# A recurrence with a rounded two-pass matmul: difference tiles kept in PSUM, a fourth seven-product block in the third pair

## The chip, the cores and the metric

The kernel runs on one core of a Trainium2 chip. The metric is device time in microseconds (us) of one execution, as the median over runs. Shorter is better.

## The reference, cut to what matters

Two stages follow each other. The first is a recurrence along 6080 positions for two batches and 256 channels; the second is a dense layer pair with an ELU between the two matrix products.

```python
# x, f_logit: (2, 6080, 256)   lower_bound: (256)
sig = 1 / (1 + exp(-f_logit))
f = lower_bound + (1 - lower_bound) * sig
for t in range(6080):
    h = f[:, t] * h + (1 - f[:, t]) * x[:, t]
    y[:, t] = h
# y as (12160, 256); w_in: (256, 2048), w_out: (2048, 256)
h = y @ w_in
g = where(h > 0, h, exp(min(h, 0)) - 1)
out = g @ w_out
```

## The kernel before

**Tiling.** Everything is held transposed, with channels on the 128 partitions. The 6080 positions are cut into twelve stretches (SIZES, of 512 except for one of 448), and each stretch is taken for both batches at once: one such *pair* of position tiles, p from 0 to 11, named by the letters a to l. The 2048 inner channels are cut into eight *blocks* of 2 x 128, so a pair has eight blocks and the kernel has 96, numbered q = 8p + j. A block is a 2 x 2 problem: two tiles of inner channels (m) by two batches (t), and it takes 2 x 2 tiles of the input's channels. Its result is four tiles g(m, t) of 128 x 512, and the second matrix product adds them into four accumulators of the pair, acc(e, t), e being the tile of output channels.

**Precision.** Each operand is split into a rounded high part and the rest (names with h and l: gh and gl, wiH and wiL, yh and yl), and a product is three passes: high by high, low by high, high by low. ScalarE makes the high part with a cast; VectorE or GpSimd subtracts it from the value for the low part (`split`, `split_sum`, `operand`).

**First product.** From the thirteenth block on (q of 12 and more) the first matmul of a block is made with seven products M1 to M7 in place of eight (`quad`, L1137). They go into three PSUM tiles, x, v and z, which share four banks in turn (pool h). M1 goes to x, M3 to v, M4 to z; ScalarE copies x to SBUF as q, VectorE adds v and z to it; M5 is added to v, M2 to z, and these two sums are the tiles (0,1) and (1,0). Each goes through ELU (`elu`, L854: Exp and Relu on ScalarE, a max and subtraction on VectorE) into the SBUF tile g. Then M7 is added to v and M6 to z, and VectorE subtracts from q in place, in the bank (steps hv and hz). What stands there now are the *difference tiles*, which become (0,0) and (1,1). They go through ELU too (steps f0 and f1), with the result written to an SBUF tile hs; from the third pair on q carries a 1, so that f0 and f1 are one Exp and one min and max. After that the bank is free.

**Second product.** In an ordinary block (`second`, L965) the four g tiles are multiplied with the output weights in 24 matmuls: g is rounded as one 1024-wide tile (step s1), hs as another (step s2, written for GpSimd, though a mark in the order can give it to VectorE). In a *wide* block this product takes seven products too, 21 matmuls (`wide_product`, L997; P1 to P7). For them VectorE forms X (a tile of g less both tiles of hs, one 1024-wide step), Y1 and Y0. The first blocks of a pair are wide, `breadth` of them (L358): none in the first two pairs, three in the third, four in each later one. A wide block needs sums of its output weights, which `combine_out` (L652) makes once per block number; those of the fourth are made during the third pair, since there the fourth block is ordinary and uses the weights as they were. `chained` (L1200) ends the wide blocks of a pair together.

**End of a pair.** `store` (L1060) moves the accumulators out. In pairs with wide blocks the parts (e, t) other than (1,1) are added by VectorE to what is there already, and (1,1) is copied with a bias; in the last pair this copy is cut in two halves, one for ScalarE and one for VectorE (L1077), and each part leaves by a DMA of its own from SyncE.

**Order.** All steps are entered in a plan with the tiles they read and write, and a list written out by hand (ORDER, L66, 5239 entries) gives the one sequence in which they are issued; each engine runs its own steps in that sequence. An entry with a ~ goes to the other of VectorE and GpSimd. Costs and due times (`cost`, `want`, `late`) were for the planner that wrote the list and do nothing at run time. Steps of VectorE that work on SBUF alone and all steps of GpSimd are chained: where the engine changes from one to the next, the later one waits for the earlier (`lock`, `port`, at the end of the kernel). Steps of VectorE with a bank among their operands are outside that chain.

Of the kernel before, what the change touches and what calls it, by code (L numbers as in the profile page):

```python
# [7 lines left out]
F32 = mybir.dt.float32  # L8
# [42 lines left out]
FULL_FROM = 3  # L51
# [306 lines left out]
def breadth(p):  # L358

    return 0 if p < WIDE_FROM else WIDE - (p < FULL_FROM)  # L360

# [91 lines left out]
def kernel(  # L453
# [397 lines left out]

    def elu(q, group, j, src, src_names, want, psum, up=False):  # L854

        n = size(q)
        cnt = len(group["tiles"])
# [557 lines left out]
```

## Time and profile before

| | us |
|---|---|
| median of 3 runs | 973.31 |
| lowest and highest of them | 973.06 and 973.47 |
| the profiled execution | 973.24 |
| its span, first to last instruction | 971.5 |
| TensorE (PE) busy | 965.7 |
| VectorE (DVE) busy | 907.6 |
| ScalarE (ACT) busy | 808.3 |
| GpSimd (POOL) busy | 424.8 |

The span is the profiled execution from its first to its last instruction; the 1.74 us around it are not in the trace. A matmul's row lasts 0.39 us while the next starts 0.23 us after it, since matmuls are pipelined. So the busy time of PE says only that it is never empty, and how dense it is must be read from the spacing of starts and from the waits. A row of a shape group gives the mean time of one instruction. "Idle before" is the time that the engine stood still just ahead of the group's instructions, with the work that ended it.

### The profile page before, as it was taken

The page shows a single profiled execution, that of the slowest core. Times are in us where ns is not written, and L with a number is a line of the kernel's source. Part 1 is how long each engine was busy: PE and PEld are TensorE (multiplying, and loading weights), DVE is VectorE, ACT ScalarE, POOL GpSimd, SP SyncE. Part 2 cuts the span into 40 slices and gives each one's busy share as a digit, 9 for nine tenths or more (in the row PEclk, how much of TensorE's full clock was granted, in tenths as well). Part 3 has the DMA queues.
Part 4 walks back from the last instruction along what each step waited for, and adds up shares of the span by engine and source line. Part 5 has one row for each costly group of instructions (what it writes and reads, how often), then busy time and mean ns, then how long its engine had stood idle before and what let it go on. Part 6 is the DMA issues. An engine that isn't in the chain of part 4 may idle for free.

```text
span 971.5 us, 12644 instructions
## 1 busy us (share of the span) xinstructions
PE 965.7 (99%) x4283; PEld 800.8 (82%) x4283; DVE 907.6 (93%) x1305; ACT 808.3 (83%) x1304; POOL 424.8 (44%) x311
## 2 busy tenths in 40 slices
PE   9999999999999999999999999999999999999998
PEld 5788999888888888888888888888888888888886
DVE  7999999999899999999999999999999999998986
ACT  7899967898789789878888988978987887897865
POOL 0231124544663652563363364256346246436622
PEclk9999999999999999999999999999999999999999
DMA  6532100120002012011111100201201201010001
GB/s 216 174 119 78 54 1 1 39 86 1 6 39 87 1 44 86 1 44 48 41 44 43 45 15 29 88 1 43 88 1 44 75 14 44 22 65 23 23 1 44
DMA packets 10145, 46.55 MB, mean 48 GB/s; under 512 B 1248, under 2 KB 1248, under 8 KB 7520
## 3 DMA queue, kind: packets, MB, share of 16 engines
q1 hardware_dynamic: 9936, 45.75, 13.3%
q8 instruction: 33, 0.54, 0.2%
q14 instruction: 32, 0.26, 0.1%
q10 hardware_dynamic: 144, 0.00, 0.0%
HBM read 33.29 MB, written 12.45 MB: 47 GB/s over the span
## 4 chain that ended last, share of the span: by engine, by line
PE 98%; DMA 1%; ACT 1%; DVE 0%; SPq 0%; issue 0%
PE o L954 51%; PE hv L835 18%; PE hz L835 18%; PE hx L835 6%; DMA gl<-fx 1%; ACT gl L521 0%; PE h(_312 L835 0%; PE h(_389 L835 0%; PE h(_315 L835 0%; PE h(_400 L835 0%; PE h(_341 L835 0%; PE h(_955 L835 0%; PE h(_948 L835 0%; PE h(_936 L835 0%; PE h(_881 L835 0%; PE h(_862 L835 0%
## 5 line engine op out<-in xcount | busy, mean ns | idle before, releaser
L508 POOL TENSOR_TENSOR gl<-g,gh 128x1024 fp32r<-128x1024 f32 (+2 forms) x92 | 178.7, 1948 | 110.9 <-ACT gh L519 18.4
L519 ACT CAST gh<-g 128x1024 fp32r<-128x1024 f32 (+2 forms) x190 | 180.1, 952 | 45.9 <-DVE g L876 19.1
L835 PE MATMUL hz<-yo,wiH 128*128 128x512 f32 (+1 forms) x504 | 193.4, 388 | 0.0
L835 PE MATMUL hv<-yo,wiH 128*128 128x512 f32 (+1 forms) x504 | 192.5, 388 | 0.0
L954 PE MATMUL o<-gh,woL 128*128 128x512 f32 (+1 forms) x526 | 162.8, 386 | 0.0
L954 PE MATMUL o<-gh,woH 128*128 128x512 f32 (+1 forms) x526 | 162.3, 386 | 0.0
L954 PE MATMUL o<-gl,woH 128*128 128x512 f32 (+1 forms) x526 | 160.0, 386 | 0.0
L525 ACT ACTIVATE e<-e 128x512 f32<-128x512 f32 (+1 forms) x202 | 125.2, 626 | 3.9
L508 DVE TENSOR_TENSOR gl<-g,gh 128x1024 fp32r<-128x1024 f32 (+1 forms) x98 | 116.5, 1192 | 1.7 <-ACT gh L519 1.1
L954 PEld LDWEIGHTS o<-gl,woH 128*128 128x128 f32 x526 | 98.6, 188 | 19.4 <-DVE gl L508 0.2
L954 PEld LDWEIGHTS o<-gh,woL 128*128 128x128 f32 x526 | 98.7, 188 | 19.1 <-POOL woL L508 0.2
L954 PEld LDWEIGHTS o<-gh,woH 128*128 128x128 f32 x526 | 98.7, 188 | 19.1 <-ACT woH L519 0.2
L835 PEld LDWEIGHTS hv<-yo,wiH 128*128 128x128 f32 x504 | 94.6, 188 | 19.0
L835 PEld LDWEIGHTS hz<-yo,wiH 128*128 128x128 f32 x504 | 94.6, 188 | 19.0
L835 PE MATMUL hz<-yo,wiL 128*128 128x512 f32 (+1 forms) x252 | 97.8, 388 | 0.0
L835 PE MATMUL hv<-yo,wiL 128*128 128x512 f32 (+1 forms) x252 | 97.7, 388 | 0.0
L508 POOL TENSOR_TENSOR yo<-raw,yo 128x512 fp32r<-128x512 f32 (+1 forms) x38 | 49.1, 1296 | 109.8 <-DVE yo L508 46.8
L519 ACT CAST yo<-raw 128x512 fp32r<-128x512 f32 (+1 forms) x147 | 88.2, 615 | 9.4 <-DVE raw L761 4.2
L508 DVE TENSOR_TENSOR yo<-raw,yo 128x512 fp32r<-128x512 f32 (+1 forms) x109 | 72.0, 683 | 1.9 <-PE o L954 1.2
L525 ACT ACTIVATE e<-hv,units 128x512 f32<-128x512 f32 x80 | 54.9, 687 | 19.7 <-DVE hv L508 18.2
L508 POOL TENSOR_TENSOR ys<-raw 128x512 f32<-128x512 f32 x29 | 37.5, 1299 | 69.0 <-DVE raw L761 35.2
L525 ACT ACTIVATE e<-hz,units 128x512 f32<-128x512 f32 x80 | 55.0, 688 | 14.6 <-DVE hz L508 13.5
(382 smaller groups left out, 2075.2 us busy)
## 6 DMA issues: line engine op xcount, KB each, us to landing
raw<-fx SPq DMA_DIRECT2D x20, 1024.0 KB, 4.8
out_t<-v SPq DMA_DIRECT2D x20, 512.0 KB, 2.6
raw<-w SPq DMA_DIRECT2D x16, 512.0 KB, 4.7
raw<-fx SPq DMA_DIRECT2D x2, 896.0 KB, 4.5
gl<-fx SPq DMA_DIRECT2D x2, 512.0 KB, 6.1
out_t<-v SPq DMA_DIRECT2D x4, 256.0 KB, 2.2
out_t<-v SPq DMA_DIRECT2D x2, 448.0 KB, 3.8
gh<-fx SPq DMA_DIRECT2D x2, 256.0 KB, 4.4
```

The lines of the kernel that those rows point to most:

```text
L508: return e, cost, lambda: engines[e].tensor_tensor(out=out_(), in0=in0(), in1=in1(), op=op)
L519: nc.scalar.copy(out=out_(), in_=in_())
L525: nc.scalar.activation(out=out_(), in_=in_(), func=func, **args)
L835: nc.tensor.matmul(out=hb(q, b), lhsT=(wiH if m == "h" else wiL)[:, i, wi], rhs=T[kind, p, name], start=(start and j == 0), stop=(j == len ...
L954: nc.tensor.matmul(out=accs[p, e, t], lhsT=lhsT, rhs=rhs, start=(c == 1), stop=(c == total(p, e, t)), skip_group_check=True,)
```

## The change

- The fourth block of the third pair becomes wide, like the first three (FULL_FROM is 2, and `breadth` gives NARROW or WIDE, both four). The weight sums of the fourth block are made with those of the others, ahead of the third pair.
- In all blocks from the thirteenth on but the very last, the ELU of the difference tiles writes its result back into the bank (`stay`). The new `split_bank` rounds them from there, each tile for itself: a 512-wide cast by ScalarE and a 512-wide subtraction by VectorE per tile (steps t0 and t1) in place of step s2.
- In wide blocks X becomes two 512-wide steps that read the banks, and Y1 reads a bank too; both are VectorE's. Y0 is now kept in a tile of g. The bank is free after the last of these steps.
- The order is written anew (5465 entries). In it the last accumulator that PE completes is (1,1), whose copy is the one in halves; before it was (0,1). The planner's numbers for the last DMAs change.

The list of the order is cut to its first line; the rest of the diff is whole.

```diff
@@ -48,7 +48,8 @@
 
 WIDE = 4
 WIDE_FROM = 2
-FULL_FROM = 3
+FULL_FROM = 2
+NARROW = 4
 NPLAIN = MP + MIXED
 SECOND = [*range(MP - MIXED, MP), *range(MP - MIXED)]
 
@@ -63,285 +64,297 @@
 
 
 ORDER = (
-    " 0 3 4 5 6 7 8 9 10 11 12 13 14 15 16 17 18 19 20 21 22 23 24 25 26 27 28 29 30 31 32 33 34 35"
...
+    " 0 33 21 26 28 34 35 43 29 31 39 12 20 36 14 40 42 37 7 19 11 51 24 52 25 5 15 30 32 13 48 4"
...
 )
@@ -357,7 +370,7 @@
 
 def breadth(p):
 
-    return 0 if p < WIDE_FROM else WIDE - (p < FULL_FROM)
+    return 0 if p < WIDE_FROM else NARROW if p < FULL_FROM else WIDE
 
 
 def place(q):
@@ -851,7 +864,7 @@
 
 
 
-    def elu(q, group, j, src, src_names, want, psum, up=False):
+    def elu(q, group, j, src, src_names, want, psum, up=False, stay=False):
 
         n = size(q)
         cnt = len(group["tiles"])
@@ -865,6 +878,8 @@
             return t
 
         def gt():
+            if stay:
+                return src()
             t = tl(group["pool"], g, [P, group.get("slots", cnt), n])
             return t.rearrange("p c n -> p (c n)") if j is None else t[:, j]
 
@@ -875,8 +890,9 @@
                 "DVE", dve_cost(width), want + 1.3,
                 lambda: nc.vector.scalar_tensor_tensor(
                     out=gt(), in0=et(), scalar=1.0, in1=src(), op0=ALU.min, op1=ALU.max,
-                ), reads=src_names + [e], writes=[(g, j)], takes=[(group["pool"], g)],
-                lock=not psum,
+                ), reads=[e] + ([] if stay else src_names),
+                writes=src_names if stay else [(g, j)],
+                takes=[] if stay else [(group["pool"], g)], lock=not psum,
             )
             return
         act(width, want, et, src, func=ACTF.Exp, reads=src_names, writes=[e], takes=[(kind, e)])
@@ -886,8 +902,9 @@
             lambda: nc.vector.scalar_tensor_tensor(
                 out=gt(), in0=src(), scalar=0.0, in1=et(), op0=ALU.max,
                 op1=ALU.subtract,
-            ), reads=src_names + [e], writes=[(g, k) for k in (range(cnt) if j is None else [j])],
-            takes=[(group["pool"], g)], lock=not psum,
+            ), reads=[e] + ([] if stay else src_names),
+            writes=src_names if stay else [(g, k) for k in (range(cnt) if j is None else [j])],
+            takes=[] if stay else [(group["pool"], g)], lock=not psum,
         )
         group["used"] = [(g, k) for k in range(cnt)]
 
@@ -907,6 +924,16 @@
         tt(eng, n * cnt, want + 1.0, lambda: tl("gl", l, [P, cnt, n], F32R), v,
            lambda: T[h].bitcast(F32), ALU.subtract, either=True, reads=rd + [h], writes=[l],
            takes=[("gl", l)])
+
+    def split_bank(q, g, j, bk, want):
+
+        n = size(q)
+        h, l = ("gh", g), ("gl", g)
+        act(n, want, lambda: tl("gh", h, [P, 2, n], F32R)[:, j], lambda: hb(q, bk),
+            reads=[bank(q, bk), h], writes=[(h, j)], takes=[("gh", h)])
+        tt("DVE", n, want + 1.0, lambda: tl("gl", l, [P, 2, n], F32R)[:, j], lambda: hb(q, bk),
+           lambda: T[h][:, j].bitcast(F32), ALU.subtract, psum=True, reads=[bank(q, bk), h, (h, j), l],
+           writes=[(l, j)], takes=[("gl", l)])
 
     def held(q, k):
 
@@ -916,8 +943,9 @@
         if k == 2:
             c = ("c", p, 2)
             return (lambda: tl("raw", c, [P, 4, n])[:, j]), [c, (c, j)], [(c, j)], [("raw", c)]
-        if k == 3:
-            return (lambda: T["hs", q][:, 0]), [("hs", q), (("hs", q), 0)], [(("hs", q), 0)], []
+        if k == 3 or (k == 1 and j >= 4):
+            g, at = ("g", q, 1), k % 3
+            return (lambda: T[g][:, at]), [g, (g, at)], [(g, at)], []
         at = 2 * (j % 2) + k
         return (lambda: tl("raw", c, [P, 4, n])[:, at]), [c, (c, at)], [(c, at)], [("raw", c)]
 
@@ -936,7 +964,9 @@
 
     def tile_parts(g, j):
 
-        return (lambda: T["gh", g][:, j], lambda: T["gl", g][:, j]), ([("gh", g)], [("gl", g)])
+        return (lambda: T["gh", g][:, j], lambda: T["gl", g][:, j]), (
+            [("gh", g), (("gh", g), j)], [("gl", g), (("gl", g), j)]
+        )
 
     accs, counts = {}, {}
 
@@ -989,7 +1019,7 @@
                         )
                 plan.add(
                     "PE", len(es) * pe_cost(n), want + 0.5 * (3 * j + pas), fn,
-                    reads=[("gl" if pas == 2 else "gh", g),
+                    reads=[("gl" if pas == 2 else "gh", g), (("gl" if pas == 2 else "gh", g), j),
                            (("wo", i), "l" if pas == 1 else "h")],
                     **both(p, t, es),
                 )
@@ -1096,10 +1126,10 @@
         if p == NP - 1:
             for e in range(KD):
                 plan.add(
-                    "SP", 0.75, want + 1.0,
+                    "SP", 0.45, want + 1.0,
                     lambda e=e: nc.sync.dma_start(
                         out=out[:, at + e * n:at + (e + 1) * n], in_=out_tile(p, t)[:, e]
-                    ), reads=[o, (o, e), *([(o, 2)] if e else [])], late=-0.6,
+                    ), reads=[o, (o, e), *([(o, 2)] if e else [])], late=-0.3,
                 )
             return
         plan.add(
@@ -1173,26 +1203,34 @@
                lambda bk=bk: hb(q, bk), ALU.subtract, psum=True, reads=[qn, bank(q, bk)],
                writes=[bank(q, bk)])
         g2 = dict(name=hs, tiles=[(0, 0), (1, 1)], pool="g")
+        stay = True and not tail
         for j, (bk, off) in enumerate((("v", 8.6), ("z", 10.9))):
-            elu(q, g2, j, lambda bk=bk: hb(q, bk), [bank(q, bk)], o(f"f{j}", off), True, up)
+            elu(q, g2, j, lambda bk=bk: hb(q, bk), [bank(q, bk)], o(f"f{j}", off), True, up, stay)
+        if stay and not w:
+            for j, (bk, off) in enumerate((("v", 13), ("z", 14))):
+                split_bank(q, hs, j, bk, o(f"t{j}", off))
+            second(q, g2, o("L2", 18))
+            return
         if not w:
             split(q, hs, "DVE" if tail else "POOL", o("s2", 15))
             second(q, g2, o("L2", 18))
             return
-        split(q, hs, "DVE", o("s2", 13))
-        c = ("c", p, i // 2)
-        at = 2 * (i % 2)
+        for j, (bk, off) in enumerate((("v", 13), ("z", 14))):
+            split_bank(q, hs, j, bk, o(f"t{j}", off))
+        x0, x0_rd, x0_wr, x0_takes = held(q, 0)
+        x1, x1_rd, x1_wr, x1_takes = held(q, 1)
         y1, y1_rd, y1_wr, y1_takes = held(q, 2)
-        x0, x0_rd, _, _ = held(q, 0)
         y0, y0_rd, y0_wr, _ = held(q, 3)
-        tt("DVE", 2 * n, o("X", 13.2), lambda: tl("raw", c, [P, 4, n])[:, at:at + 2],
-           lambda: T[g][:, 1:2].to_broadcast([P, 2, n]), lambda: T[hs], ALU.subtract,
-           reads=[g, (g, 1), hs, (hs, 0), (hs, 1), c], writes=[(c, at), (c, at + 1)],
-           takes=[("raw", c)])
-        tt("DVE", n, o("Y1", 15), y1, lambda: T[hs][:, 1], x0, ALU.subtract, either=True,
-           reads=[hs, (hs, 1), *x0_rd], writes=y1_wr, takes=y1_takes)
+        for j, (x, wr, takes, bk) in enumerate(
+            ((x0, x0_wr, x0_takes, "v"), (x1, x1_wr, x1_takes, "z"))
+        ):
+            tt("DVE", n, o("X", 13.2), x, lambda: T[g][:, 1], lambda bk=bk: hb(q, bk),
+               ALU.subtract, psum=True, reads=[g, (g, 1), bank(q, bk), *(x0_rd if j < 1 else x1_rd)],
+               writes=wr, takes=takes)
+        tt("DVE", n, o("Y1", 15), y1, lambda: hb(q, "z"), x0, ALU.subtract, psum=True,
+           reads=[bank(q, "z"), *x0_rd, *y1_rd], writes=y1_wr, takes=y1_takes)
         tt("DVE", n, o("Y0", 15.5), y0, lambda: T[g][:, 0], y1, ALU.subtract, either=True,
-           reads=[g, (g, 0), hs, *y1_rd], writes=y0_wr)
+           reads=[g, (g, 0), *y1_rd], writes=y0_wr)
         split_sum(q, 3, o("sY0", 16))
         wide_product(q, 0, 1, 2, tile_parts(hs, 1), o("P3", 17))
         wide_product(q, 1, 0, A22, sum_parts(q, 3), o("P4", 21))
@@ -1330,7 +1368,8 @@
                 for k in range(breadth(WIDE_FROM)):
                     combine_out(k, plan.at(f"bo{k}", base(WIDE_FROM * MP - 1.5 + 0.4 * k)))
             if q == WIDE_FROM * MP + WIDE - 1 and FULL_FROM > WIDE_FROM:
-                combine_out(WIDE - 1, plan.at(f"bo{WIDE - 1}", base(q + 3)))
+                for k in range(NARROW, WIDE):
+                    combine_out(k, plan.at(f"bo{k}", base(q + 3)))
             if q == NPLAIN - 1:
                 for k, i in enumerate(SECOND[:MIXED]):
                     combine(i, plan.at(f"b{i}", base(MP + MIXED + 3.802 + 1.953 * k)))
```

## Rows read from the trace of the kernel before

**Rows 1.** Page, busy time: engine, busy us (share of span), instructions.

```profile
PE 965.7 (99%) x4283; PEld 800.8 (82%) x4283; DVE 907.6 (93%) x1305; ACT 808.3 (83%) x1304; POOL 424.8 (44%) x311
```

**Rows 2.** Page, chain of waits that ended last, shares of the span by engine.

```profile
PE 98%; DMA 1%; ACT 1%; DVE 0%; SPq 0%; issue 0%
```

**Rows 3.** Windows: stretch, its us, busy us (instructions) by engine, granted clock, DMA.

```profile
0.00:40.00 40.00, 37.96 (x149) 25.68 (x150) 31.61 (x48) 32.27 (x52) 6.60 (x12) 1.00 0.61 211
...
80.00:120.00 40.00, 40.00 (x188) 34.95 (x187) 39.78 (x72) 38.44 (x70) 8.83 (x13) 1.00 0.21 78
...
120.00:160.00 40.00, 40.00 (x204) 37.16 (x203) 39.41 (x64) 29.08 (x54) 11.63 (x10) 1.00 0.00 0
...
960.00:971.50 11.50, 7.70 (x34) 6.03 (x33) 6.51 (x9) 2.54 (x4) 0.80 (x1) 0.98 0.24 92
...
600.00:680.00 80.00, 80.00 (x355) 66.26 (x354) 76.68 (x111) 66.50 (x106) 36.16 (x25) 1.00 0.11 40
```

**Rows 4.** Waits of PE, whole span: who for whom, us, times, longest.

```profile
PE hzeros L1234 <- POOL wsH L1223: 1.2, 1, 1.2
PE h(_240 L820 <- DVE raw L761: 0.6, 1, 0.6
PE h(_247 L820 <- DVE raw L761: 0.2, 1, 0.2
```

**Rows 5.** Timeline of PE, first product and last matmuls: start us, us, instruction.

```profile
9.76 1.10 PE L820 MATMUL h(_240<-raw,v 128*128 128x512 f32 x2 [0.61 <-DVE raw L761]
...
966.63 0.39 PE L954 MATMUL o<-gh,woL 128*128 128x512 f32 x1
966.86 0.39 PE L954 MATMUL o<-gh,woH 128*128 128x512 f32 x1
967.08 0.39 PE L954 MATMUL o<-gl,woH 128*128 128x512 f32 x1
967.31 0.39 PE L954 MATMUL o<-gh,woL 128*128 128x512 f32 x1
```

**Rows 6.** Groups by shape, VectorE: name, shapes, count, busy us, mean ns, idle before.

```profile
L508 DVE TENSOR_TENSOR gl<-g,gh 128x1024 fp32r<-128x1024 f32 x85 | 103.2, 1218 | 1.7 <-ACT gh L519 1.1 <-POOL yo L508 0.3 <-POOL raw L508 0.2
...
L508 DVE TENSOR_TENSOR yo<-raw,yo 128x512 fp32r<-128x512 f32 x104 | 68.9, 686 | 1.9 <-PE o L954 1.2 <-ACT e L525 0.2
...
L508 DVE TENSOR_TENSOR hv<-q,hv 128x512 f32<-128x512 f32 x80 | 55.4, 692 | 6.1 <-PE hv L835 5.6
...
L508 DVE TENSOR_TENSOR q<-q,hv 128x512 f32<-128x512 f32 x80 | 54.7, 683 | 7.7 <-PE hv L835 3.3 <-ACT q L525 2.4 <-ACT raw L525 0.4
...
L508 DVE TENSOR_TENSOR raw<-g 128x1024 f32<-128x1024 f32 x39 | 47.6, 1221 | 1.1
```

**Rows 7.** Groups by shape, GpSimd.

```profile
L508 POOL TENSOR_TENSOR gl<-g,gh 128x1024 fp32r<-128x1024 f32 x50 | 120.2, 2412 | 103.8 <-ACT gh L519 18.4 <-DVE yo L508 16.8 <-ACT e L525 15.7
```

**Rows 8.** Groups by shape, ScalarE.

```profile
L519 ACT CAST gh<-g 128x1024 fp32r<-128x1024 f32 x135 | 141.1, 1049 | 36.6 <-DVE g L876 19.1 <-DVE g L886 7.3 <-PE o L954 5.3
...
L525 ACT ACTIVATE q<-hx 128x512 f32<-128x512 f32 x80 | 47.5, 593 | 6.5 <-PE hx L835 6.1
```

**Rows 9.** Timeline of VectorE and of SyncE's DMA issues, the end.

```profile
965.25 0.48 DVE L1077 TENSOR_SCALAR v<-o,cs 128x256 f32<-128x256 f32 x1 [1.04 <-PE o L954]
...
967.74 0.69 DVE L508 TENSOR_TENSOR v<-v,o 128x512 f32<-128x512 f32 x1 [0.67 <-PE o L954]
...
966.26 2.52 SPq L1100 DMA_DIRECT2D out_t<-v  x4
```

**Rows 10.** Timeline of PE's weight loads, two waits in the head.

```profile
17.55 0.30 PEld L954 LDWEIGHTS o<-g,v 128*128 128x128 f32 x2 [0.63 <-DVE v L595]
...
20.92 0.19 PEld L835 LDWEIGHTS h(_312<-yo,wiH 128*128 128x128 f32 x1 [0.50 <-ACT wiH L519]
```

**Rows 11.** Waits, all engines: VectorE for ScalarE.

```profile
DVE g L886 <- ACT e L525: 9.6, 18, 2.2
```

568 rows, old and new, of the table ORDER are left out of this document.

## The prediction

> **What bounds the kernel now.** I began with busy time. TensorE is busy 99% of the span, VectorE 93%, ScalarE 83%, GpSimd 44% [rows 1]. A busy PE need not be a fed PE, so the chain of waits came next: 98% of it is PE, and no other engine has more than 1% [rows 2]. Then the stretches: an 80 us stretch in the middle holds 80.00 us of PE time and 355 matmuls at the full granted clock [rows 3], and in the whole span PE waited three times for named work, 2.0 us in all, two of them at its first products [rows 4]. The timeline of the last matmuls gives the price of one: starts at 966.63, 966.86, 967.08 and 967.31, so 0.227 us each [rows 5]. At that price 80 us hold 353, and a stretch also counts matmuls that overlap its edges. So from about 40 us on, the time is the number of matmuls times 0.227 us. The rest is a head (the first product starts at 9.76) and a tail of some 4 us behind the last matmul [rows 5]. The other engines matter only if one of them stops feeding PE. VectorE is the near one: 39.8 of 40 us early on and 76.7 of 80 in the middle [rows 3].
>
> **Fourth wide block in the third pair.** A block whose second matmul takes eight products issues 24 matmuls for it, one with seven issues 21. One block changes, so three matmuls go: 3 x 0.227 = 0.68 us, all on the path, since PE has no idle time there. This is the only edit that takes work off PE. The head's warming matmuls are the same fifty, one of them placed between the first products.
>
> **Difference tiles in PSUM.** I counted operations by engine in the two written orders (a ~ moves one to the other of VectorE and GpSimd) and priced them by the rows. Before, 84 roundings of the (0,0),(1,1) tiles are one 1024-wide ScalarE cast at 1.05 us [rows 8] and one 1024-wide subtraction, 50 on VectorE at 1.22 [rows 6] and 34 on GpSimd at 2.41 [rows 7]; X is 39 at 1.22. After, 83 of them are two 512-wide casts and two 512-wide subtractions that read the bank, all on VectorE (they are offered to no other engine); X is 80 of 512 and Y1 40, also on VectorE. No row has these forms. The nearest VectorE row reads a bank and writes SBUF, 0.683 us; one that writes the bank takes 0.692, one from SBUF 0.686 [rows 6]: bounds of 0.68 and 0.69, and I take 0.683. The nearest cast is the ScalarE copy out of a bank, 0.593 [rows 8].
>
> On VectorE the subtractions grow from 50 x 1.22 = 61 us to 166 x 0.683 + 1.2 = 115, X from 48 to 55, Y1 from 16 x 0.69 = 11 to 27: plus 77 us. The new order hands back to GpSimd what still reads SBUF only: operand sums and roundings (75 on VectorE become 36), s1 roundings (35 wide ones become 21), sum roundings, Y0 and k4: minus 69 us. All told VectorE's changed steps go from 298 to 307 us, GpSimd's from 393 to 418, ScalarE's from 267 to 281. Added to [rows 1]: VectorE 916 of 971 (94%), GpSimd 451, ScalarE 822. None reaches PE. Where VectorE is fullest, the early pairs (39.8 and 39.4 of 40 us [rows 3]), the sum of its work up to the 712th matmul is 170 us in both orders, each width at its price from the rows, although the fourth block's weight sums move forward by about 100 matmuls: all seven of their steps that either engine could take are GpSimd's now, the widest of which was VectorE's.
>
> The kernel lets VectorE work on SBUF alone and GpSimd work only in turns. VectorE steps in that queue fall from 538 to 342 and handovers between the two from 261 to 173, so that wait shrinks. I give it nothing, as PE does not wait for it.
>
> [...]
>
> **Longer hold of the banks.** Four banks serve x, v and z of successive blocks. In the written orders a wide block's v bank is held for 61 matmuls on average instead of 50, z for 59 instead of 45; other blocks 80 and 75 instead of 77 and 73. With x, which is short, a wide block needs some 130 of the 4 x 42 = 168 bank-matmuls of its time. Between the last reader of a bank and the matmul that retakes it stand 7 matmuls (median) instead of 12, none at all in 24 cases instead of 7. With the seven of before PE never waited on a bank, so I cost it at nothing; the cover is the other block's second matmuls, and without it each case costs at most one VectorE step, 0.69 us.
>
> **Tail.** PE now ends on accumulator (1,1), which ScalarE and VectorE copy in halves, instead of (0,1), which VectorE adds in one piece. The half takes 0.48 us, the piece that ends now 0.69 [rows 9]: minus 0.21 us. The piece is then due three matmuls earlier and its DMA is issued first; four issues take 2.52 us [rows 9], so the last may queue, and the gain may be nothing. I take 0.2. On the other side GpSimd now rounds the last block's first tiles (2.41 us [rows 7]) with their first reader 16 matmuls behind the last product: up to 0.5 us lost if it is late. The changed costs and lateness of the output DMAs only steer the planner.
>
> **Head.** ScalarE's casts change places among the first blocks. PE waited there 0.63 us for VectorE at 17.55 and 0.50 for ScalarE at 20.92 [rows 10]. One cast moves ahead of these, one behind: between minus 0.5 and plus 0.5, taken as nothing.
>
> **Sum.** Span 971.5 - 0.68 - 0.2 = 970.6. The profiled execution took 973.24, 1.74 more than its span, and lies 0.07 below the median: 973.24 - 0.88 = 972.4.
>
> **Rivals.** A measurement can tell about 0.2% from no change, so faster is below 971.4 and slower above 975.3.
>
> *PE stays fed* (0.60): 972.4, from 971.8 to 973.0 by the head's and the tail's bounds.
>
> *The rearranged ends cost more than the matmuls give* (0.21): head late by 0.5, tail by 0.5 and without its gain, some banks late: 972.4 + 0.5 + 0.7 = 973.6, up to 974.9. For it: every step of the new order has a new neighbour. Against it: the ends have few steps.
>
> *ScalarE and VectorE in turns on one bank* (0.15), on the other side. Before, the readers of a difference tile follow from each other: subtract, Exp, min/max. After, the cast on ScalarE and X or Y1 on VectorE want the same bank and need nothing of each other. If they can't read at once, VectorE stops for up to 0.59 us per bank [rows 8], and behind it are queued the next block's q sums, on which its products M5 and M2 wait. VectorE already loses time so: 18 waits for an Exp, 9.6 us [rows 11]. VectorE has 3.3 us left of 80 [rows 3], 2.6 with the added 0.7; eight such banks per pair at 0.59 are 4.7. What overflows, 2.1 us in each of ten pairs, would give 972.4 + 21 = 993; half the waits, 2.4, just fit. It decides the sign from 2.9 us in all, 0.07 us per wide block: I price it at 0.2 us a block, 972.4 + 8 = 980. Against it: other ready steps stand between the tile's two readers in many places of the order.
>
> [...] No row of before has two engines free to read one bank, so nothing here shows it yet.
>
> *The head's stalls go too* (0.04): the two waits of products in [rows 4], 0.8, and those of [rows 10], 1.1, on top of the forecast: 972.4 - 1.9 = 970.5. More cannot go, since PE's work stays.
>
> **How the numbers follow.** Faster 0.04, slower 0.15, same 0.81. The range reaches from 971.3 to 974.9: it leaves out most of the two outer cases, 0.19.
>
> **What would show it.** PE 4280 matmuls, no waits beyond the head, 80 us stretches with 80.00 of PE; VectorE near 916 us, GpSimd near 451, ScalarE near 822; subtractions and X at 0.68 with a bank as source; the last VectorE step a half of 0.48. PE waiting for VectorE on hv or hz, or VectorE's X and Y1 waiting for gh on ScalarE by some tens of us, would prove me wrong.

## The result, and the profile after

| | before | after |
|---|---|---|
| median, us | 973.35 | 987.63 |
| lowest and highest | 973.06 and 973.47 | 987.47 and 987.83 |
| span of the profiled execution | 971.5 | 985.7 |

The change makes the kernel slower: the ratio is 1.0147, with a 95% interval from 1.013 to 1.0165. That is 14.3 us more than before, 15.2 above the forecast and 12.7 above the upper end of the range. Two of the executions behind the figures below, one of 1634.01 us of the kernel before and one of 3484.78 us of the kernel with the cast later, took far longer than all others of their kernels and are left out.

The page of after, with its span, its busy times (to [rows 1]) and the chain's shares by engine (to [rows 2]):

```profile
span 985.7 us, 12822 instructions
...
PE 973.4 (99%) x4280; PEld 797.3 (81%) x4280; DVE 907.2 (92%) x1395; ACT 812.5 (82%) x1391; POOL 451.6 (46%) x351
...
PE 85%; DVE 9%; ACT 3%; issue 2%; DMA 0%; POOL 0%; ACTq 0%; DVEq 0%; POOLq 0%
```

The three matmuls are gone, and no engine but GpSimd (46% of the span, 44% before) is fuller than it was. But the chain, 98% PE before, now runs over VectorE for 9% and ScalarE for 3%. Windows of after (stretch, us, busy us and instructions of PE, PEld, VectorE, ScalarE, GpSimd, granted clock, DMA):

```profile
600.00:680.00 80.00, 79.44 (x347) 64.39 (x346) 74.64 (x116) 66.47 (x116) 41.53 (x29) 1.00 0.11 40
840.00:880.00 40.00, 38.18 (x166) 30.68 (x165) 34.69 (x54) 33.82 (x58) 17.25 (x12) 1.00 0.16 53
```

The second of these stretches in the kernel before:

```profile
840.00:880.00 40.00, 40.00 (x178) 33.15 (x177) 39.06 (x55) 36.45 (x58) 12.63 (x9) 1.00 0.16 53
```

Twelve matmuls fewer in 40 us are 12 x 0.227 = 2.7 us lost there, and VectorE and ScalarE did less in the same time as well. So none of these engines became a bound; they wait for each other. For whom, the view of waits of after tells (who, for whom, us in all, times, longest; in the order PE, PEld, VectorE, ScalarE):

```profile
PE o L984 <- ACT gh L532: 3.6, 6, 1.0
...
PE o L984 <- DVE v L521: 0.8, 2, 0.5
...
PEld o L984 <- ACT gh L532: 8.5, 12, 1.4
...
DVE g L902 <- ACT e L538: 13.5, 19, 2.8
DVE gl L521 <- ACT gh L532: 8.9, 16, 0.7
DVE raw L521 <- ACT gh L532: 5.6, 11, 1.1
...
ACT gh L532 <- DVE raw L521: 22.3, 22, 1.7
```

The last line is the new one. gh is the high part that ScalarE casts out of a difference tile's bank; raw is X or Y1, which VectorE forms out of the same bank. Neither uses the other's result, yet the casts waited 22.3 us for X and Y1, X and Y1 waited 5.6 us for casts, and PE and its weight loads then waited for gh. Each waits for a signal of the other: by these waits the program lets one of the two engines at a time into a bank, in the written order. (VectorE's wait for an Exp, 9.6 us in [rows 11], is 13.5 now; it hardly goes down in the fast variants below either.)

One such place in the timeline of after, VectorE first, then ScalarE, then PE:

```profile
768.23 0.69 DVE L891 SCALAR_TENSOR_TENSOR hz<-e,hz 128x512 f32<-128x512 f32 x1
768.83 0.69 DVE L521 TENSOR_TENSOR gl<-hv,gh 128x512 fp32r<-128x512 f32 x1
769.43 0.69 DVE L521 TENSOR_TENSOR raw<-g,hv 128x512 f32<-128x512 f32 x1
770.15 0.69 DVE L521 TENSOR_TENSOR raw<-hz,raw 128x512 f32<-128x512 f32 x1
771.49 0.69 DVE L521 TENSOR_TENSOR raw<-g,hz 128x512 f32<-128x512 f32 x1 [0.65 <-ACT gh L532]
...
768.82 0.61 ACT L538 ACTIVATE e<-hv 128x512 f32<-128x512 f32 x1
770.88 0.58 ACT L532 CAST gh<-hz 128x512 fp32r<-128x512 f32 x1 [1.45 <-DVE raw L521]
...
770.14 0.39 PE L984 MATMUL o<-gh,woL 128*128 128x512 f32 x1
771.51 0.50 PE L984 MATMUL o<-gh,wsL 128*128 128x512 f32 x1 [0.98 <-ACT gh L532]
```

The difference tile in hz is finished at 768.92, and ScalarE is free from 769.43. Its cast of hz starts only at 770.88, behind Y1 (raw<-hz,raw), because Y1 stands ahead of it in the written order. Y1 itself came late, since VectorE had two other steps first. Then X (raw<-g,hz) waits 0.65 us for the cast, and PE starts a matmul 1.37 us behind the one before instead of 0.227.

Worked out from the starts of all matmuls after 35 us (what a start comes later than 0.227 us after the one before, where that is more than 0.043): 0.25 us in 3 gaps before, 13.25 us in 59 gaps after. Gaps below that size add 1.7 us, the tail 0.3, and the three matmuls take off 0.7: 13.0 + 1.7 + 0.3 - 0.7 = 14.3, and the spans differ by 14.2.

### The profile page after: what moved, and what is told of

It reads as the page before. It is cut to its first block, busy times and chain, and to the rows that moved or that the text cites. A ratio compares the mean times of both kernels' runs of the same rounds, so it can differ in the third digit from the quotient of the medians.

```text
span 985.7 us, 12822 instructions
## 1 busy us (share of the span) xinstructions
PE 973.4 (99%) x4280; PEld 797.3 (81%) x4280; DVE 907.2 (92%) x1395; ACT 812.5 (82%) x1391; POOL 451.6 (46%) x351
## 4 chain that ended last, share of the span: by engine, by line
PE 85%; DVE 9%; ACT 3%; issue 2%; DMA 0%; POOL 0%; ACTq 0%; DVEq 0%; POOLq 0%
PE o L984 45%; PE hv L848 15%; PE hz L848 14%; PE hx L848 5%; DVE raw L521 2%; ACT e L538 2%; DVE q L521 1%; DVE gl L521 1%; DVE g L902 1%; ACT gh L532 1%; DVE hv L891 1%; DVE hz L891 1%; DVE hv L521 1%; DVE v L521 1%; DVE hz L521 0%
## 5 line engine op out<-in xcount | busy, mean ns | idle before, releaser
L521 POOL TENSOR_TENSOR gl<-g,gh 128x512 fp32r<-128x512 f32 (+2 forms) x74 | 133.0, 1798 | 130.1 <-ACT gh L532 68.9
L984 PE MATMUL o<-gh,woL 128*128 128x512 f32 (+1 forms) x520 | 159.0, 387 | 0.9 <-DVE v L521 0.8
L984 PE MATMUL o<-gh,woH 128*128 128x512 f32 (+1 forms) x520 | 158.9, 387 | 0.8 <-ACT gh L532 0.8
L984 PE MATMUL o<-gl,woH 128*128 128x512 f32 (+1 forms) x520 | 157.2, 387 | 0.0
L521 POOL TENSOR_TENSOR yo<-raw,yo 128x512 fp32r<-128x512 f32 x70 | 90.2, 1297 | 85.1 <-PE o L984 25.3
L532 ACT CAST gh<-g 128x1024 fp32r<-128x1024 f32 (+2 forms) x107 | 93.4, 877 | 15.2 <-DVE g L902 12.2
L532 ACT CAST yo<-raw 128x512 fp32r<-128x512 f32 (+1 forms) x150 | 90.5, 618 | 4.8 <-DVE raw L774 1.9
L521 POOL TENSOR_TENSOR ys<-raw 128x512 f32<-128x512 f32 x43 | 55.7, 1300 | 71.9 <-DVE raw L774 53.0
L538 ACT ACTIVATE e<-hv 128x512 f32<-128x512 f32 (+1 forms) x88 | 52.3, 594 | 23.3 <-PE hv L848 20.1
L532 ACT CAST gh<-hv 128x512 fp32r<-128x512 f32 (+1 forms) x83 | 48.6, 585 | 24.7 <-DVE raw L521 13.5
L538 ACT ACTIVATE e<-hz,units 128x512 f32<-128x512 f32 x80 | 55.3, 691 | 14.2 <-DVE hz L521 13.3
```

The source lines that it names most:

```text
L521: return e, cost, lambda: engines[e].tensor_tensor(out=out_(), in0=in0(), in1=in1(), op=op)
L532: nc.scalar.copy(out=out_(), in_=in_())
L538: nc.scalar.activation(out=out_(), in_=in_(), func=func, **args)
L984: nc.tensor.matmul(out=accs[p, e, t], lhsT=lhsT, rhs=rhs, start=(c == 1), stop=(c == total(p, e, t)), skip_group_check=True,)
```

## The experiments

The theory is that ScalarE's cast and VectorE's X and Y1 take turns on a bank by these signals, and that the loss comes from the one that is ready having to wait for the one that isn't. The rivals are the longer hold of the banks, the price of reading a bank at all, and the rearranged ends.

**The cast leaves the bank.** In wide blocks ScalarE casts from another tile, but not before the difference tile is finished, so that it starts on the same condition. Its high part is then of other data, so this kernel serves the timing alone. Every queue stays as it is. The lines that add this wait for the difference tile are not shown.

```diff
-        act(n, want, lambda: tl("gh", h, [P, 2, n], F32R)[:, j], lambda: hb(q, bk),
+        src = (lambda: T["g", q, 1][:, 1]) if wide(q) else (lambda: hb(q, bk))
+        act(n, want, lambda: tl("gh", h, [P, 2, n], F32R)[:, j], src,
...
```

> The changed kernel, but in wide blocks ScalarE's cast of a difference tile reads an SBUF tile of the same size (a tile of g) in place of the bank, and still waits for the step that completes the difference tile. So that high part is of other data. Order, number of steps and the hold of the banks are the same; only the second free reader of a bank is gone. Turns (cast and X or Y1 made to wait for each other on one bank cost the 13 us of PE's stalls): 972.5 to 975.5, PE's stalls under 3 us, no wait of a cast on X or Y1. Load (the new split of work over the engines makes results late): 986 to 989. Hold (banks come free too late): 986 to 988.

Measured 973.38 us, ratio to before 1.0003 (0.9993 to 1.0012). The cast's wait for raw is gone. Of VectorE's waits for gh, that of the subtraction for its own cast is left (4.4 us, 8.9 in after) and one of 0.4; PE has none, and its weight loads one of 0.3. Waits of this kernel and the stretch shown above:

```profile
DVE g L902 <- ACT e L538: 13.3, 20, 2.8
...
DVE gl L521 <- ACT gh L532: 4.4, 10, 0.7
```

```profile
840.00:880.00 40.00, 40.00 (x178) 33.15 (x177) 36.99 (x55) 35.30 (x61) 19.40 (x14) 1.00 0.15 53
```

The whole loss hangs on the pair of readers. In the written order the subtraction, X and Y1 still hold the banks here as far as in the change, so the longer hold cost nothing by itself (973.38 us, 973.35 before). Whether it is the taking of turns or the cast's reading of a bank as such, this kernel does not tell; the next one does.

**Only who goes first.** Again every engine's queue stays as it is. Of the two readers of a bank the one goes first in the written order that was ready first in the kernel above; 18 of the 80 banks of wide blocks differ. The place of the timeline above is one of them:

```diff
-Y1 (VectorE), cast of hz (ScalarE), X (VectorE)
+cast of hz (ScalarE), Y1 (VectorE), X (VectorE)
```

> Every engine keeps its queue; only which of two readers of a difference tile's bank goes first is changed, in 18 of 80 banks, to the one that was ready first in the kernel whose casts read another tile. Theory (ScalarE and VectorE take turns on a bank, and the written order made the ready one wait): the casts' waits for raw, 22.3 us, fall below 6, PE's lost time from 13.3 us to 2 to 5, time 975 to 979. Rival (a second reader costs its time whichever goes first): waits only change sides, 986 to 988.

Measured 977.45 us, ratio 1.0044 (1.0029 to 1.0059). The same Exp and cast in this kernel's timeline, 5 and 7 us earlier by now, and the waits of casts for raw:

```profile
763.63 0.60 ACT L539 ACTIVATE e<-hv 128x512 f32<-128x512 f32 x1
764.12 0.59 ACT L533 CAST gh<-hz 128x512 fp32r<-128x512 f32 x1
```

```profile
ACT gh L533 <- DVE raw L522: 3.0, 9, 0.6
```

The cast follows the Exp at once. Ten of the fourteen us come back with no operation changed: the price is not one per second reader, it depends on who goes first.

**The other way.** In 33 banks the cast goes one reader later than in the change, queues unchanged.

> Every engine keeps its queue; in 33 of 80 banks of wide blocks the cast, which went ahead of X or Y1 in the changed kernel, is written one reader later. Theory (the written order of the two decides the loss): the casts' waits for raw rise from 22 us to 50 to 80, and the time from 987.6 to 1000 to 1020. Rival (a second reader costs the same whichever goes first): 986 to 989.

Measured 1017.64 us (the median of three), ratio 1.0454 (1.0435 to 1.0473), both figures within what the theory expected:

```profile
ACT gh L533 <- DVE raw L522: 66.6, 50, 2.7
...
PE o L985 <- ACT gh L533: 19.7, 20, 2.0
```

**Half of it.** Only the casts of z banks leave their bank (the lines that add the wait are again not shown).

```diff
-        src = (lambda: T["g", q, 1][:, 1]) if wide(q) else (lambda: hb(q, bk))
+        src = (lambda: T["g", q, 1][:, 1]) if wide(q) and bk == "z" else (lambda: hb(q, bk))
...
```

> Only the cast of the z bank (tile (1,1)) of a wide block reads another tile; the v bank keeps its two readers. Of the casts' waits in the changed kernel about 13 us stand at v banks and 9 at z banks. Theory (each turn costs where it stands): 979 to 984. Rival (z with its three readers makes nearly all of it): 973 to 976.

Measured 979.82 us, ratio 1.0069 (1.0054 to 1.0084). The v banks keep their turns, and with them 13.6 us of waiting casts, as counted beforehand; this kernel takes 6.4 us more than the first experiment. So v and z share the loss.

**The tail.** In the change the last accumulator is copied in halves, by ScalarE and VectorE. Here VectorE copies it in one piece, once on top of the retimed order and once on top of the first experiment.

> As e5_turns_retimed, with the last accumulator copied by VectorE in one piece instead of in halves by ScalarE and VectorE. Theory (the halves take turns too, 0.47 and 0.50 one behind the other): from the last matmul's start to the last DMA issue 1.14 us instead of 1.44, 0.3 us faster than e5_turns_retimed. Rival (the halves run side by side): 0.2 us slower.

> As e2_cast_elsewhere (in wide blocks the cast reads another tile, so the high part is that of other data), with the last accumulator copied by VectorE in one piece. Theory (without turns, and with the end's two halves gone, the change gives what its three matmuls are worth less small gaps): 973.0 to 973.2, 0.3 below e2_cast_elsewhere, within 0.1 of before. Rival (halves side by side are quicker): 973.5 or more.

Measured 977.17 us (0.28 below the retimed order) and 972.94 us (0.44 below the first experiment; ratio to before 0.9998, 0.9988 to 1.0008). The timeline of the end of after, and of the retimed kernel with one piece:

```profile
981.21 0.39 PE L984 MATMUL o<-gl,woH 128*128 128x512 f32 x1
981.64 0.47 ACT L538 ACTIVATE v<-o,cs 128x256 f32<-128x256 f32 x1 [5.03 <-PE o L984]
...
982.14 0.48 DVE L1107 TENSOR_SCALAR v<-o,cs 128x256 f32<-128x256 f32 x1 [0.50 <-ACT v L538]
```

```profile
971.14 0.39 PE L985 MATMUL o<-gl,woH 128*128 128x512 f32 x1
971.57 0.75 DVE L1104 TENSOR_SCALAR v<-o,cs 128x512 f32<-128x512 f32 x1
```

The halves lie one behind the other, 0.50 of VectorE's wait being ScalarE's half. They end 1.41 us after the last matmul's start, the one piece 1.18. Here the two halves of one bank on two engines were slower than one piece on one.

The change with ScalarE copying in one piece, run once:

> The changed kernel, with the last accumulator (1,1) copied by ScalarE in one piece instead of in two halves by ScalarE and VectorE. From the start of the last matmul to the end of the span it was 4.47 us. If the halves take turns on the bank (0.47 and then 0.48), one piece of 0.68 shortens that by 0.2 to 0.35. If they could run side by side, it would be longer by 0.2.

It took 988.4 us. The copy itself was quick, from 981.87 to 982.56, 1.11 us after the last matmul's start. Yet 5.1 us lay between that start and the end, 4.5 in after. One execution can't say why, and the two kernels above answer the question better.

**Is the retimed order the best of its kind?** What is left in the one-piece version, 977.17 against 972.94, I put down to banks that both want at nearly the same time: each side still waits some us for the other (3.0 and 4.7). This is argued, not shown. Two more kernels shift such cases to one side: cast first only where it was ready over 0.35 us earlier, and cast first even where it was ready 0.45 us later.

> As e8_retimed_one_piece, with the cast put first only where it was ready over 0.35 us ahead of X or Y1 in the kernel whose casts read another tile; 11 of 80 banks differ. If what remains there (4 us against before) stems from VectorE, the fuller engine, waiting for casts: 975 to 976.9. If from ScalarE waiting: 977.3 to 979.

> As e8_retimed_one_piece (977.2), with the cast put first also where it was ready up to 0.45 us behind X or Y1; 8 of 80 banks differ, the other way than in e10_vector_first. If a cast that waits is still what costs there: 975.5 to 976.9. If VectorE's waits for casts now weigh as much: 977.0 to 979.

Measured 979.39 and 982.74 us, both slower than 977.17. With VectorE favoured, casts wait 14.3 us (3.0 in the one-piece version) for 2.2 us more time, just above the second of the expected ranges. With the cast favoured, VectorE's X and Y1 wait 11.2 us (4.7) for 5.6 us more, which is beyond either expectation: 6.5 us more of VectorE's waiting cost 5.6. That VectorE, the fuller engine (92% of that kernel's span, ScalarE 83%), has less time to give would explain it; it is not shown. Waits of the latter kernel:

```profile
DVE raw L522 <- ACT gh L533: 11.2, 19, 1.1
...
ACT gh L533 <- DVE raw L522: 0.5, 2, 0.3
```

The experiments side by side (waits in us; X and Y1 are the raw of the waits):

| kernel | casts for X, Y1 | X, Y1 for casts | time |
|---|---|---|---|
| cast elsewhere, one piece | 0 | 0 | 972.94 |
| before | none | none | 973.35 |
| cast elsewhere | 0 | 0 | 973.38 |
| retimed, one piece | 3.0 | 4.7 | 977.17 |
| retimed | 3.0 | 4.7 | 977.45 |
| VectorE favoured, one piece | 14.3 | 1.5 | 979.39 |
| z casts elsewhere | 13.6 | 0.7 | 979.82 |
| cast favoured, one piece | 0.5 | 11.2 | 982.74 |
| after | 22.3 | 5.6 | 987.63 |
| cast later | 66.6 | 3.3 | 1017.64 |

**Three that told less.** X and Y1 leave the bank instead of the cast, and read an SBUF tile:

```diff
-            tt("DVE", n, o("X", 13.2), x, lambda: T[g][:, 1], lambda bk=bk: hb(q, bk),
+            tt("DVE", n, o("X", 13.2), x, lambda: T[g][:, 1], lambda: T[g][:, 0],
```

> In wide blocks the cast reads the bank as in the changed kernel, and X and Y1 read the first tile of g in SBUF instead of the banks (so X and Y1 hold other data). Theory (turns between the two): whichever reader leaves, the wait goes: 973 to 974. Rival (a cast out of the bank, or the longer hold of the bank, is what costs): 985 to 988.

Measured 1003.36 us, outside both ranges. The waits between casts and X are gone here too, but the edit brought a cost of its own. First the group of X by shape, then one of its steps in VectorE's timeline, then GpSimd's timeline beside it:

```profile
L521 DVE TENSOR_TENSOR raw<-g 128x512 f32<-128x512 f32 x80 | 70.9, 891 | 4.3 <-POOL g L521 4.3
```

```profile
534.58 1.74 DVE L521 TENSOR_TENSOR raw<-g 128x512 f32<-128x512 f32 x1 [0.87 <-POOL g L521]
...
534.50 1.27 POOL L521 TENSOR_TENSOR yo<-raw,yo 128x512 fp32r<-128x512 f32 x1
```

X now reads SBUF alone, and takes 1.74 us beside a GpSimd step that began just before it. Over all 80, the 49 that overlapped no GpSimd step averaged 0.685 us, the 31 that did 1.216. So this kernel swapped one conflict for another and does not decide the question; the first experiment does.

The cast directly behind ELU (in 66 of the 80 banks of wide blocks), and the subtraction ahead of X and Y1 (in 72):

```diff
-ELU's step, ..., X, Y1, cast, subtraction
+ELU's step, cast, ..., subtraction, X, Y1
```

> The changed kernel with its whole work, in another order in wide blocks: the cast stands straight behind the step that completes the difference tile, and VectorE's subtraction stands ahead of X and Y1 on that bank, with one other VectorE step between. Both readers still use the bank, but the cast no longer queues behind X and Y1. Turns: 975 to 981, the waits of casts on X and Y1 (22 us) down to under 5. Load: 986 to 989. Hold: 986 to 988, since the banks are held no shorter.

Measured 1013.37 us, ratio 1.0412 (1.0397 to 1.0428). The casts' waits for X and Y1 fell to 3.1 us as expected, but the time rose. This one changes the queues as well, and other waits grew: casts for the ELU step in front of them (5.9 us for hz and 8.8 for hv in after), and VectorE's subtraction for its cast (8.9 in after):

```profile
ACT gh L533 <- DVE hz L892: 27.7, 37, 1.9
ACT gh L533 <- DVE hv L892: 21.4, 29, 1.2
...
DVE gl L522 <- ACT gh L533: 15.6, 25, 1.5
```

To have the turn early was not enough: the casts, put close behind their source, made ScalarE's queue wait 49.1 us for it (27.7 and 21.4), 14.7 in after.

Difference tiles kept in PSUM in wide blocks only:

```diff
-        stay = True and not tail
+        stay = w and not tail
```

> The changed kernel, with difference tiles kept in PSUM in wide blocks only; in ordinary blocks they go to SBUF as before and are rounded as one 1024-wide tile, by VectorE. So 78 bank holds are short again, 156 subtractions and casts become 78 of double width, and all pairs of free readers stay. Turns: 984 to 989. Load: VectorE has some 6 us less to do and ScalarE 5, 979 to 984. Hold: about half the stalls, 979 to 982.

Measured 1086.72 us, ratio 1.1167 (1.115 to 1.1183), and no answer: the order that I merged for it gave GpSimd 70 of the 1024-wide roundings, 166.7 us, where after has 31, and PE waited for them:

```profile
PE o L980 <- POOL gl L517: 37.5, 20, 6.7
```

What ordinary blocks add alone stays open. The first experiment bounds it: with turns taken out of wide blocks only, nothing is left to explain.

## Why the prediction was wrong, step by step

**The bound and the matmuls: right.** 4280 matmuls at the same 0.227 us. In the first experiment the stretch from 35 us to the last matmul is 0.25 us shorter than before: the 0.68 forecast, less 0.43 in gaps, none of them over 0.11.

**Durations in PSUM: right.** Groups by shape of after, VectorE and ScalarE:

```profile
L521 DVE TENSOR_TENSOR gl<-hv,gh 128x512 fp32r<-128x512 f32 x79 | 54.1, 686 | 6.2 <-ACT gh L532 5.3
...
L532 ACT CAST gh<-hv 128x512 fp32r<-128x512 f32 x79 | 46.5, 588 | 24.3 <-DVE raw L521 13.5 <-DVE hv L891 8.8 <-PE o L984 1.2
```

0.686 and 0.588 against 0.683 and 0.593 taken. X out of a bank took 0.684 (hv) and 0.682 (hz). From SBUF alone it took no less: 0.685 where it left the bank, in the 49 that overlapped no GpSimd step.

**Sums by engine: GpSimd right, the other two 9 us too high.** GpSimd 451.6 (451 forecast), VectorE 907.2 (916), ScalarE 812.5 (822). The term that was mis-sized is the price of cutting a step in two: a row's duration is not what a step adds to a queue. In the timeline of after VectorE's 0.69 us steps start at 768.23, 768.83 and 769.43, 0.60 apart, so they overlap by 0.09, and busy time counts an overlap once. Added up row by row, VectorE's durations did grow, from 989.2 us to 1002.1, and ScalarE's from 886.8 to 902.5; their busy times went from 907.6 to 907.2 and from 808.3 to 812.5. It changed nothing, since neither engine was the bound.

**Longer hold at nothing: right**, as the first experiment shows.

**Tail: wrong in sign**, -0.2 forecast, +0.3 measured (last matmul's start to the end of the span: 4.15 us before, 4.47 after). The step took the half's 0.48 from [rows 9] as if the two halves ran side by side. The trace of before shows that they don't. In ScalarE's timeline at its end, the other half of the copy:

```profile
965.76 0.47 ACT L525 ACTIVATE v<-o,cs 128x256 f32<-128x256 f32 x1 [2.82 <-DVE v L1077]
```

VectorE's half of the same accumulator ran from 965.25 [rows 9]; ScalarE's waited for it.

**The missing term and the ranking of the rivals: here the prediction failed.** The step that failed is *PE stays fed*: the sum has no term for ScalarE's cast and VectorE's X and Y1 having to take turns on a bank. That term measured 14.25 us (987.63 in the change, 973.38 with the cast elsewhere), 0.36 for each of 40 wide blocks. Without it and with the end in one piece the time is 972.94, within the 971.8 to 973.0 that *PE stays fed* gave. *ScalarE and VectorE in turns on one bank* is what happened, between the 980 that I priced, at 0.2 us a block, and the 993 that I gave as its far end. It had a chance of 0.15 for two reasons, both wrong. The first was the sentence "No row of before has two engines free to read one bank": the row just shown is one, two engines with nothing to ask of each other except the bank, and one waits. For these programs it settles the "if they can't read at once": the second reader waits for a signal of the first. What the chip does without that wait was not tried.

The second reason was "other ready steps stand between the tile's two readers in many places". I weighed this as a chance and counted nothing. Counted by the readiness in the trace of the first experiment, which I didn't have then, the order puts first the reader that is ready later in 18 of 80 banks. And the price, "0.59 us per bank" against VectorE's slack of 3.3 us in 80, looked at the wrong engine. Most of the waiting, 22.3 of 27.9 us, was ScalarE's, the engine with time to spare, for up to 1.7 us at once, since it waits not for a step but for VectorE's queue ahead of that step. The sign that I named, X and Y1 waiting for gh by some tens of us, came to 5.6. PE felt the casts' waits where gh is the operand of its next product; how much of its 13.25 us came that way, and how much through other steps held up in the queues of VectorE (9% of the chain of after) and ScalarE, was not separated. ScalarE's slack over a stretch, 13.5 us of 80 in the middle before [rows 3] and in after, did not hide these waits.

*The rearranged ends* were not it: the tail's 0.3 us is all that they cost. *The head*: the first product starts at 9.71 us, 9.76 before [rows 5], and by 35 us PE has started one matmul more than before.

**What the change could give at best.** With the turns out of the way and the end in one piece, 972.94: within 0.1% of before, and by other data in the cast. The best order that I found for the change as it is, 977.17, is still 0.4% slower than before.

## What to carry to other kernels

Before a tile stays in PSUM, list every reader of its bank by engine: two engines that ask nothing of each other may ask for the bank, and here the order in which they were written decided who waited (casts 22.3 us and X and Y1 5.6 in after, 66.6 and 3.3 with the cast later). Copying such a tile to SBUF, as the kernel before does, buys that independence: no cast waited there for X or Y1, nor X or Y1 for a cast. If a bank must have two readers, write first the one that is ready first (here worth 10 us of 14, with no operation changed), favour neither engine beyond that (2.2 us lost with VectorE favoured, 5.6 with the cast), and don't cut one bank's copy into halves for two engines (0.28 and 0.44 us lost).

## What the runs showed of the hardware

Where X left the bank, a VectorE step with two sources in SBUF took 0.685 us alone and up to 1.81 beside a GpSimd step. Whichever of the two began first kept its time there, unless it was held up by an earlier one itself. In the rows shown with that experiment it was GpSimd's step (1.27, and 1.30 on average in after), and X ended at 536.32, 0.55 behind its end at 535.77. So it was in 23 of the 26 X that began during a GpSimd step: each ended 0.55 behind it. Where the GpSimd step began during an X, the GpSimd step was the one that grew; the eight of them that were 512 wide took 1.35 to 1.76 us and ended 1.14 to 1.16 behind the X. One such pair:

```profile
593.44 0.68 DVE L521 TENSOR_TENSOR raw<-g 128x512 f32<-128x512 f32 x1
...
593.58 1.70 POOL L521 TENSOR_TENSOR gl<-g,gh 128x512 fp32r<-128x512 f32 x1 [7.21 <-DVE gl L521]
```

The kernel's chain keeps such steps apart: in the traces of before and after no VectorE step with both sources in SBUF overlaps a GpSimd step. A step that reads a bank needed no place in it: the 47 of the 80 X of after that overlapped a GpSimd step averaged 0.682 us, the other 33 0.683. Moving its operand to SBUF was not free, 0.891 on average.
